# The first layer's attention segments in another order, with a refitted plan

## The chip, the cores and the metric

One core of one Trainium2 chip runs the whole kernel. The metric is device time in microseconds (us), the median of several runs.

## The reference

Four layers work on 2048 tokens of width 512 and add to x in turn: A, B, A, B, with the same weights both times. A is local attention (8 keys at distances 0, 2, ..., 14), B is full attention with 32 query heads that share one key head and one value head of width 16.

```python
x = A_x
x = x + _A_ref(_layernorm(x, axis=-1), A_wqkv, A_wo)
x = x + _B_ref(_layernorm(x, axis=-1), B_wq, B_wk, B_wv, B_wo)
x = x + _A_ref(_layernorm(x, axis=-1), A_wqkv, A_wo)
x = x + _B_ref(_layernorm(x, axis=-1), B_wq, B_wk, B_wv, B_wo)
...
scores = jnp.einsum("bhqd,bkd->bhqk", q, k) * (Dh ** -0.5)   # in _B_ref
p = _softmax(scores, axis=-1)
o = jnp.einsum("bhqk,bkd->bhqd", p, v)
```

## The kernel before, in words

The tokens are cut into four chunks of 512. "Layer" in the title means a pair A + B, numbered l = 0 and 1. For each chunk, `chunk` writes down the A part (layer norm, projections q, k, v, banded attention in "units", output projection) and then `b_in`, which makes B's keys (`kb`, into KAB) and queries (`qb`, into QT) of that chunk. These are operations with dependencies and estimated durations.

B's attention is a stream of tiles: one tile is 128 keys by 512 queries of one head group. A tile's scores are a matmul of 32 rows (line 1842). Its exponential is then taken by one of two engines: two tiles at a time on ACT (`exp`, line 1857, from a PSUM slot "st"), or one at a time on DVE (`copy`, line 1861, from a PSUM bank "dv", to a buffer t), from which POOL makes two shifted copies per tile (`do_pass`, line 1867). Then come matmuls with the values (line 1878), one for a tile that ACT took and three for a tile that DVE took. A tile may go either way, so ACT and DVE share the tile work.

The stream's order is written in `Net.order`. Each entry is (l, query chunk, key tiles), and it stands for eight segments, one for each pair (t, a) of head groups. When a query chunk meets its keys in several entries, the partial result of a segment is kept in X: the first part is copied out of PSUM (line 1897, DVE, or line 1895, ACT), every later part is added to X (line 1898, DVE alone). If another query chunk comes between, X goes to DRAM (line 1905) and comes back (line 1917). When a query chunk has met all keys, `rows` normalizes it, `out_rows` projects it, and its A part of the next layer is put into the plan.

A planner (`Sched.plan`) decides at build time in which order each engine issues all this. It takes for each engine the candidate with the smallest key: earliest start plus a bias. The biases (`PRM`, `Stream.BIAS`) are overridden from certain segments on by the table `PHASES`. `emit` writes the instructions in the planned order, and `chain` ties each to the one before on its engine. Some instructions are written without that tie: all but the last of the selects that build a band mask (`build_band_mask`, lines 1073 to 1079), and all but the last memset of `build_ones` (line 1094). Their place on POOL is decided when the program is built, around the tied ones.

DVE and POOL instructions that are marked with `port` are also tied to each other, across both engines, in the order of the plan: the later one waits for the earlier one by semaphore.

```python
if self.sched and self.sched.lock:
    order_after(self.tc, inst, self.tail.get("port" + {"dve": "pool", "pool": "dve"}[key]))
    self.tail["port" + key] = inst
```

Marked so are, in the start of the kernel: on DVE the layer norm's shift (line 1377), its normalization (line 1399) and the band mask of a unit (line 1585); on POOL the copies that spread A's values (line 1529).

Of the kernel before, what the change touches and what calls it, by code (L numbers as in the profile page):

```python
# [410 lines left out]
def outproj_tm(ctx, tc, o_tm, wo_sb, x_sb, ident, S, tag):  # L411
# [5 lines left out]
    for qt in range(NT):  # L417
# [27 lines left out]

PHASES = {
    0: ({
        "ex": -306.6, "add": 235.5, "vp": 291.7, "c3": -107.5, "dve": -147.3,
    }, {
        "dq": 159.2, "aq": -134.4,  # L450
    }),
    3: ({
        "age": 0.04278, "c2": -145.8,
    }, {
        "mmi": 48.87,
    }),
    6: ({
        "age": 0.05331,
    }, {
        "pv": 216.7, "mmpt": 17.28, "mmi": 4.008,  # L460
    }),
    9: ({
        "back": 1023,
    }, {
        "vec": 517, "mmi": -6.329, "aux": -147.2, "vec2": 217.1, "vech": 0.1986,
    }),
    12: ({}, {
        "few": 56.89, "slotv": 26.53,
    }),
    15: ({  # L470
        "age": 0.03159, "dve": -47.39,
    }, {
        "pv": 261.3, "copy": 144.9, "nt": -10.19, "mmpt": 38.35, "aux": -79.09, "exq": 23.25, "vecp": -40.88,
        "slotv": 38.3,
    }),
    18: ({
        "scale": 323.2,
    }, {}),
    21: ({}, {}),
    24: ({  # L480
        "recip": 623.4,
    }, {
        "batch": 20.29, "copy": -9.763,
    }),
    27: ({
        "scale": 268.7,
    }, {
        "npt": -0.5879, "ni": -9.215, "nt": 13.06, "mmq": 38.47,
    }),
    30: ({  # L490
        "age": 0.04279, "wpd": -0.07726, "mm_a": 405.5, "evacX": 93.91, "recip": 107.6, "c4": -43.8,
    }, {
        "pv": 222.9, "mmq": 11.47, "mmi": 42.58, "vec2": 155.6, "dq": -60.88,
    }),
    33: ({
        "age": 0.04061, "norm": 35.21, "aexp": -62.26, "ex": -204.6, "scale": -303.2, "dve": -86.78,
    }, {
        "vec": 419.9, "mmq": 7.941, "mmpt": 27.1, "mmi": 5.567, "aux": 49.57, "dq": 24.8,
    }),
    36: ({  # L500
        "age": 0.03932, "mm_a": 485, "norm": 69.12, "v0": 1080, "score": -231.1, "recip": 241.3, "scale": 350.2,
        "c5": 163.2,
    }, {
        "act": -182.5, "pv": 260.2, "npt": 3.996, "mmq": 38.14, "mmpt": -11.57, "mmi": 4.721, "vec2": 168.4,
        "vecp": -43.99, "slotv": 3.272,
    }),
    39: ({
        "age": 0.0403, "mask": -43.5, "c5": 75.84, "c6": 39.43,
    }, {
        "vec": 480.2, "batch": 23.44, "npt": 0.3429, "nt": -20.7, "mmq": 18.85, "mmpt": 25.18, "vec2": 184.8,  # L510
        "vecp": -74.21, "slotv": 31.5,
    }),
    42: ({
        "age": 0.04324, "mm_a": 502.6, "dmat": 736.3, "scale": 293.2, "c5": 79.56,
    }, {
        "vec": 466.2, "copy": 101.1, "ni": -11.61, "mmpt": 14.5,
    }),
    45: ({
        "age": 0.01627, "score": -187.1,
    }, {  # L520
        "pv": 267.3, "npt": 8.481, "nt": 11.16, "mmpt": 11.35, "mmi": 13.75, "aux": 15.46, "exq": -80.66,
    }),
    48: ({
        "mm_a": 410, "add": 91.46, "recip": 43.8, "c6": 51,
    }, {
        "pv": 276.6, "copy": 105.8, "npt": 2.948, "mmq": -2.49, "mmpt": 22.57, "mmi": 30.08, "vec2": 122.7,
        "dq": 38.09,
    }),
    51: ({
        "sc": 153.2,  # L530
    }, {
        "batch": 20.02, "ni": -21.41, "mmq": 8.641,
    }),
    54: ({}, {
        "aux": -58.57,
    }),
    57: ({
        "wd": 0.1189, "st": 130.9, "sc": 15.74,
    }, {
        "pv": 245.9, "batch": 19.21, "slotv": 20.79,  # L540
    }),
    60: ({
        "age": 0.041, "mm_a": 499.4, "act": 371.2, "dve": -34.12,
    }, {
        "vec": 446.8, "pv": 295.7, "pv_in": 180.4, "batch": 22.72, "npt": 30.29, "ni": -15.73, "nt": -40.24,
        "mmq": 6.584, "mmpt": 54.33, "mmi": 30.31, "exq": -41.21, "aq": -117.4, "vecp": -63.63,
    }),
    63: ({
        "act": -171.6,
    }, {  # L550
        "vec": 373.4,
    }),
    66: ({
        "recip": 149, "scale": 435,
    }, {}),
    69: ({
        "recip": 140.1,
    }, {
        "ni": -9.089, "nt": 22.53, "vecp": -73.11,
    }),  # L560
    72: ({
        "scale": 553.6,
    }, {
        "vec": 288.3, "pv": 129.3, "copy": 179.8, "vecp": 18.01,
    }),
    75: ({
        "mm_a": 483.7, "evacX": -26.18, "scale": 119.6,
    }, {
        "pv": 211.9, "npt": -16.9, "ni": -26.06,
    }),  # L570
    78: ({}, {}),
    81: ({
        "age": 0.04053, "mm_a": 487.1, "scale": 327.4,
    }, {
        "copy": 136.4, "ni": -11.35, "nt": -29.96, "mmpt": 87.33, "mmi": 4.607,
    }),
    84: ({}, {}),
    87: ({
        "mm_a": 54.57, "recip": 392.7,
    }, {  # L580
        "pv": 199.8, "vecp": -109.8,
# [12 lines left out]

# [532 lines left out]
class Net:  # L1127
# [1228 lines left out]
```

## Time and profile before

| what | us |
| --- | --- |
| median of 3 runs (lowest, highest) | 1377.09 (1376.57, 1378.69) |
| the profiled execution | 1378.62 |
| its span, first to last instruction | 1376.9 |
| busy: PE, ACT, DVE, POOL | 1340.7, 1318.4, 1292.0, 938.0 |

The profiled execution is 1.5 us over the median of the runs, and 1.7 us of it lie outside the span. Three engines are busy for 94% to 97% of the span. PE's share says less than it seems, since its matmuls overlap (up to four run side by side) and a busy PE may have room.

### The profile page before, as it was taken

Reading aid. Unit: us, or ns where it says so; the run is one execution under the profiler, and the core shown is the slowest. Engines: PE = TensorE matmul, PEld = TensorE weight load, DVE = VectorE, ACT = ScalarE, POOL = GpSimd, SP = SyncE. Lnnn points to the kernel's source line nnn. Section 1 sums busy time; section 2 is a strip of 40 time slices with the busy share of each in tenths; the row PEclk is TensorE's granted clock in tenths of the full one; section 3 lists DMA queues with packets and bytes.
Section 4 is the critical chain, followed back from the end, with each engine's and each line's share of the span. In section 5 each row is a group of like instructions: output and inputs, shape, how many; then the busy total and the mean of one; then the engine's idle time right before and its main releaser. Section 6 shows DMA issues by size and latency. Waiting matters only on the chain.

```text
span 1376.9 us, 48313 instructions
## 1 busy us (share of the span) xinstructions
PE 1340.7 (97%) x19729; PEld 455.5 (33%) x19729; DVE 1292.0 (94%) x2280; ACT 1318.4 (96%) x1593; POOL 938.0 (68%) x1225
## 2 busy tenths in 40 slices
PE   8999999999999999999999999999999999999996
PEld 5534343222224332433334333422222222222222
DVE  7988879999998899999999999899999999999996
ACT  7899989999999999999999999999999999999995
POOL 5137466788866657775668556677876778886884
PEclk9999999999999999999999999999999999999999
DMA  5012222011111110111101011121022200001000
GB/s 157 6 36 63 71 46 76 15 37 30 42 43 29 18 36 18 24 24 26 25 15 27 31 48 40 36 66 50 27 57 61 58 30 6 22 6 43 14 14 26
DMA packets 120014, 51.63 MB, mean 37 GB/s; under 512 B 98600, under 2 KB 104872, under 8 KB 119784
## 3 DMA queue, kind: packets, MB, share of 16 engines
q1 hardware_dynamic: 118920, 46.63, 13.7%
q8 instruction: 156, 2.56, 0.8%
q10 hardware_dynamic: 864, 1.84, 0.4%
q14 instruction: 74, 0.61, 0.1%
HBM read 22.90 MB, written 11.52 MB: 25 GB/s over the span
## 4 chain that ended last, share of the span: by engine, by line
PE 66%; ACT 17%; DVE 7%; POOL 5%; issue 4%; DMA 1%; SPq 0%; POOLq 0%; DVEq 0%; ACTq 0%
PE o L1878 28%; PE st L1842 22%; ACT pt L1857 14%; DVE t L1861 3%; PE y L1336 3%; PE qb L1336 2%; PE dv L1842 2%; ACT units L1857 2%; PE k L1336 2%; PE q L1336 2%; PE v L1677 2%; POOL i_pair L1867 1%; POOL i L1867 1%; POOL v L1693 1%; DMA region<-in_A_x_dram 1%
## 5 line engine op out<-in xcount | busy, mean ns | idle before, releaser
L1857 ACT ACTIVATE pt<-st 128x1024 bf16<-128x1024 f32 x1116 | 1076.6, 1125 | 19.4 <-PE dv L1842 11.0
L1861 DVE TENSOR_SCALAR t<-dv 128x512 int16<-128x512 f32 x1546 | 966.7, 681 | 29.4 <-PE dv L1842 24.3
L1867 POOL INT64_ADD i<-t x618 | 507.9, 829 | 250.9 <-DVE t L1861 80.3
L1867 POOL INT64_ADD i_pair<-t x414 | 340.5, 826 | 142.8 <-DVE t L1861 52.5
L1842 PE MATMUL st<-QT,KAB 32*128 32x512 bf16 x1300 | 252.5, 382 | 5.2 <-ACT pt L1857 2.4
L1842 PE MATMUL st<-QT,region 32*128 32x512 bf16 x1250 | 243.8, 381 | 5.6 <-ACT pt L1857 2.5
L1842 PE MATMUL dv<-QT,region 32*128 32x512 bf16 x798 | 244.2, 383 | 0.1
L1878 PE MATMUL o<-pt,VEa 128*32 128x512 bf16 x1138 | 235.9, 385 | 0.2 <-DVE t L1861 0.2
L1878 PE MATMUL o<-pt,region 128*32 128x512 bf16 x1094 | 235.2, 387 | 0.0
L1842 PE MATMUL dv<-QT,KAB 32*128 32x512 bf16 x748 | 232.3, 382 | 0.5 <-DVE t L1861 0.5
L1878 PE MATMUL o<-i,region 128*32 128x512 f16 x954 | 226.8, 386 | 0.3 <-POOL i L1867 0.3
L1878 PE MATMUL o<-t,region 128*32 128x512 f16 x798 | 207.0, 386 | 0.0
L1878 PE MATMUL o<-i,VEd 128*32 128x512 f16 x898 | 201.5, 384 | 0.1
L1878 PE MATMUL o<-t,VEd 128*32 128x512 f16 x748 | 196.1, 385 | 0.1
L1857 ACT ACTIVATE units<-st 128x1024 bf16<-128x1024 f32 x159 | 179.0, 1126 | 2.9 <-PE dv L1842 2.8
L1878 PE MATMUL o<-i_pair,region 128*32 128x512 f16 x642 | 170.2, 385 | 0.4 <-POOL i_pair L1867 0.4
L1842 PEld LDWEIGHTS <-region 32*128 32x128 bf16 x2048 | 81.0, 91 | 240.6 <-issue 236.6
L1842 PEld LDWEIGHTS <-KAB 32*128 32x128 bf16 x2048 | 78.0, 90 | 239.6 <-issue 233.2
L1878 PE MATMUL o<-i_pair,VEd 128*32 128x512 f16 x598 | 149.1, 384 | 0.1
L1878 PEld LDWEIGHTS <-region 128*32 128x32 f16 (+1 forms) x3644 | 71.0, 94 | 155.0 <-issue 150.8
L1878 PEld LDWEIGHTS <-VEd 128*32 128x32 f16 x2244 | 68.2, 94 | 81.6 <-issue 75.6
L1878 PEld LDWEIGHTS <-VEa 128*32 128x32 bf16 x1300 | 57.3, 94 | 60.8 <-issue 58.1
(193 smaller groups left out, 1268.7 us busy)
## 6 DMA issues: line engine op xcount, KB each, us to landing
xkd<-X SPq DMA_DIRECT2D x32, 256.0 KB
X<-xkd SPq DMA_DIRECT2D x32, 256.0 KB
lb<-rcd SPq DMA_DIRECT2D x31, 256.0 KB
X<-X SPq DMA_DIRECT2D x124, 32.0 KB
k<-oncA SPq DMA_DIRECT2D x96, 32.0 KB
w_sb<-in_A_wqkv_dram ACTq DMA_DIRECT2D x4, 384.0 KB
region<-in_A_x_dram SPq DMA_DIRECT2D x3, 512.0 KB
out_dram<-w_sb SPq DMA_DIRECT2D x3, 512.0 KB
```

The costliest lines, as they stand in the source:

```text
L1336: self.chain("pe", self.nc.tensor.matmul(st["ps"][g:g + 32], lhsT=lhsT[:, g:g + 32], rhs=rhs, start=first and n == 0, stop=last and n == l ...
L1677: self.chain("pe", nc.tensor.matmul(ps[0][32 * h:32 * h + 32, b], lhsT=B.xnT.t[:, kt, at:at + 32], rhs=wv[:, kt, h, :, :], start=(kt == 0) ...
L1693: self.chain("pool", nc.gpsimd.tensor_copy(out=vv[rows, 4 * n:4 * n + 4, :, 16 * h:16 * h + 16].rearrange("p b g d -> p (b g) d"), in_=st. ...
L1842: self.chain("pe", self.nc.tensor.matmul(out, lhsT=self.KAB[l][32 * g:32 * g + 32, a, kt * 128:(kt + 1) * 128], rhs=self.QT[32 * g:32 * g ...
L1857: self.chain("act", self.nc.scalar.activation(out=self.pt[pt][:, 0:n, :], in_=self.st.pop(key)[:, 0:n, :], func=AF.Exp, scale=E_SCALE))
L1861: self.chain("dve", self.nc.vector.tensor_scalar(out=self.t[buf][:, r, :].bitcast(I16), in0=self.dv[bank][:], scalar1=-U_BIAS, scalar2=U_B ...
L1867: self.chain("pool", self.nc.gpsimd.int64_add(words(self.i[out]), words(self.t[buf]), J_OFF[j] * 0x0001000100010001))
L1878: self.chain("pe", self.nc.tensor.matmul(self.o[bank][32 * g:32 * g + 32, :], lhsT=lhsT, rhs=rhs, start=first, stop=last, tile_position=(0 ...
```

## The change

The order of segments of the first layer's first two query chunks is another one. Before: chunk 0 on keys 0, chunk 1 on keys 0 and 1, chunk 0 on keys 1 to 3, chunk 1 on keys 2 and 3. After: chunk 0 on keys 0, chunk 0 on keys 1, chunk 1 on keys 0 to 2, chunk 0 on keys 2 and 3, chunk 1 on keys 3. There is one entry more, so eight segments more, and the segment numbers behind it move up by eight. The table PHASES has other numbers throughout, those in force from the first instruction on among them. The new table is 29 lines longer, so line n of the kernel before that stands behind it is line n + 29 after.

```diff
 PHASES = {
     0: ({
-        "ex": -306.6, "add": 235.5, "vp": 291.7, "c3": -107.5, "dve": -147.3,
+        "norm": 328.5, "vcopy": 15.72, "ln": -57.44, "ex": -364.2, "on": 22.28, "c1": -185.7, "c3": -110.5,
+        "vfirst": -1066, "dve": -150.6,
     }, {
...
     def order(self):
         k = lambda a, b: range(4 * a, 4 * b)
-        return [(0, 0, k(0, 1)), (0, 1, k(0, 2)), (0, 0, k(1, 4)), (0, 1, k(2, 4)),
+        return [(0, 0, k(0, 1)), (0, 0, k(1, 2)), (0, 1, k(0, 3)), (0, 0, k(2, 4)), (0, 1, k(3, 4)),
                 (0, 2, k(0, 4)), (0, 3, k(0, 4)),
                 (1, 0, k(0, 2)), (1, 1, k(0, 3)), (1, 0, k(2, 4)), (1, 1, k(3, 4)), (1, 2, k(0, 4)), (1, 3, k(0, 4))]
```

**First place: POOL in the start, where A's values of chunk 0 are spread.** Line 1529 (1558 after) copies the values, two instructions for each of four blocks. `bandones` is the pattern for the narrow band mask (line 1073: its memset, 1077 and 1079: its selects), `ones` a constant. Before:

```order
L1529 COPY v<-oncA 64x32x16 x2
L1094 MEMSET ones_114 32x16 x3
L1529 COPY v<-oncA 64x32x16 x4
L1073 MEMSET bandones 128x40
L1529 COPY v<-oncA 64x32x16 x2
L1077 AFFINE_SELECT bandones<-bandones 32x8
L1077 AFFINE_SELECT bandones<-bandones 32x32
```

After:

```order
L1558 COPY v<-oncA 64x32x16 x2
L1123 MEMSET ones_114 32x16 x3
L1102 MEMSET bandones 128x40
L1106 AFFINE_SELECT bandones<-bandones 32x8
L1106 AFFINE_SELECT bandones<-bandones 32x32
...
L1108 AFFINE_SELECT bandones<-bandones 32x8
L1558 COPY v<-oncA 64x32x16 x6
L1567 COPY ks<-k 128x512
```

The memset and 15 selects stood behind all eight copies (the memset behind six), and stand now between the second copy and the third.

**Second place: DVE at the same time.** Line 1311 (1340) casts values, 1084 (1113) makes the wide band mask's bits, 1377 (1406) is the layer norm's shift for chunk 1, 1399 (1428) normalizes rows of chunk 1 (to a borrowed buffer `pt`), 1313 (1342) scales keys, 1416 (1445) copies transposed rows, 1585 (1614) masks the first unit. The brackets name the semaphores that an instruction waits for. Before:

```order
L1311 CAST oncA<-v 128x512 [waits PE_49] x3
L1084 TENSOR_SCALAR bandmask_102<-bandones 128x72 [waits Pool_49]
L1377 SCALAR_TENSOR_TENSOR sm_201<-sm_201 128x2 [waits DVE_49,Activation_49,Pool_49]
L1311 CAST q_183<-q 128x512 [waits PE_49]
L1313 TENSOR_SCALAR k<-k,kmask 128x8x64 [waits PE_49]
L1416 COPY QT<-pT 128x4x128 [waits PE_49] x2
L1585 TENSOR_TENSOR units<-units,bandmask_102 128x576 [waits DVE_49,Activation_49,Pool_49]
```

After:

```order
L1340 CAST oncA<-v 128x512 [waits PE_49]
L1113 TENSOR_SCALAR bandmask_102<-bandones 128x72 [waits Pool_49]
L1406 SCALAR_TENSOR_TENSOR sm_201<-sm_201 128x2 [waits DVE_49,Activation_49,Pool_49]
L1428 TENSOR_SCALAR pt_157<-region,sm_201 128x512 [waits DVE_49]
L1428 TENSOR_SCALAR pt_157<-region,sm_201 128x512 [waits Pool_49]
L1340 CAST q_183<-q 128x512 [waits PE_49]
L1342 TENSOR_SCALAR k<-k,kmask 128x8x64 [waits PE_49]
L1445 COPY QT<-pT 128x4x128 [waits PE_49] x2
L1614 TENSOR_TENSOR units<-units,bandmask_102 128x576 [waits DVE_49,Activation_49,Pool_49]
```

Two casts went to ACT, and two normalizations came from ACT. By the counts that the semaphores are waited for, the shift waited for the sixth copy on POOL and waits now for the second; the second normalization is new here and waits for the fourth copy; the unit's mask waits for the eighth copy in both; the third copy waits for the first normalization, the fifth for the second.

**Third place: ACT while the A part of chunk 3 projects q and k** (line 1308, 1337 after: casts of the projections; line 1857, 1886 after: exponentials). Before:

```order
L1857 ACTIVATE pt_155<-st 128x1024
L1308 CAST oncA<-k 128x2x256
L1857 ACTIVATE pt_154<-st 128x1024
L1308 CAST oncA<-k 128x2x256
L1308 CAST q_184<-q 128x512
L1308 CAST oncA<-k 128x2x256
L1308 CAST q_185<-q 128x512
L1308 CAST oncA<-k 128x2x256
L1857 ACTIVATE pt_157<-st 128x1024
```

After:

```order
L1337 CAST oncA<-k 128x2x256
L1886 ACTIVATE pt_155<-st 128x1024
L1886 ACTIVATE pt_154<-st 128x1024
L1337 CAST q_184<-q 128x512
L1886 ACTIVATE pt_157<-st 128x1024
L1886 ACTIVATE pt_158<-st 128x1024
L1337 CAST q_185<-q 128x512
L1337 CAST oncA<-k 128x2x256
L1886 ACTIVATE pt_156<-st 128x1024
```

Of the eight projections, the last six stood on PE in one piece without a score between them (five of their casts follow each other on ACT); now the last three do, and exponentials stand between the others.

## Rows read from the trace of the kernel before

**Rows 1.** The page: its span, and busy time of each engine with its share.

```profile
span 1376.9 us, 48313 instructions
PE 1340.7 (97%) x19729; PEld 455.5 (33%) x19729; DVE 1292.0 (94%) x2280; ACT 1318.4 (96%) x1593; POOL 938.0 (68%) x1225
```

**Rows 2.** Stretches: length, busy us of PE, PEld, DVE, ACT, POOL, clock, DMA.

```profile
123.00:230.50 107.50, 104.96 (x2092) 41.77 (x2080) 90.09 (x165) 102.04 (x138) 64.05 (x91) 1.00 0.24 58
411.50:750.00 338.50, 334.63 (x5512) 118.21 (x5504) 320.73 (x559) 329.76 (x394) 229.86 (x296) 1.00 0.12 24
750.00:967.00 217.00, 213.22 (x3399) 73.39 (x3396) 202.78 (x355) 210.46 (x257) 146.28 (x188) 1.00 0.17 45
280.00:320.00 40.00, 39.19 (x418) 10.74 (x414) 39.99 (x68) 40.00 (x45) 32.79 (x41) 1.00 0.13 38
```

**Rows 3.** The chain that ended last, 13 to 40 us: start, us, what.

```profile
17.81 0.62 POOL v L1529
...
18.65 0.81 ACT pt L1396
...
21.98 0.88 PE k L1336 x16
...
25.38 0.68 DVE units L1585
```

**Rows 4.** Timeline of POOL in the start: start, us, line, operation, tiles, [idle before].

```profile
14.02 1.27 POOL L1529 COPY v<-oncA 64x512 bf16<-64x512 bf16 x2 [6.36 <-DVE sm L1377]
15.35 0.46 POOL L1094 MEMSET ones<- 32x16 bf16 x3
15.85 2.57 POOL L1529 COPY v<-oncA 64x512 bf16<-64x512 bf16 x4
...
20.02 1.84 POOL L1077 TENSOR_SCALAR_AFFINE_SELECT bandones<-bandones 32x8 bf16<-32x8 bf16 x7
...
22.44 1.29 POOL L1079 TENSOR_SCALAR_AFFINE_SELECT bandones<-bandones 32x32 bf16<-32x32 bf16 x6
```

**Rows 5.** Timeline of DVE in the start.

```profile
13.79 1.88 DVE L1311 CAST oncA<-v 128x512 bf16<-128x512 f32 x3
15.58 0.17 DVE L1084 TENSOR_SCALAR bandmask<-bandones 128x72 int16<-128x72 bf16 x1
18.45 0.16 DVE L1377 SCALAR_TENSOR_TENSOR sm<-sm 128x2 f32<-128x2 f32 x1 [2.69 <-POOL v L1529]
18.53 0.69 DVE L1311 CAST q<-q 128x512 bf16<-128x512 f32 x1
19.13 0.74 DVE L1313 TENSOR_SCALAR k<-k,kmask 128x512 bf16<-128x512 f32 x1
...
20.60 0.79 DVE L1585 TENSOR_TENSOR units<-units,bandmask 128x576 int32<-128x576 int32 x1
21.32 0.44 DVE L1399 TENSOR_SCALAR pt<-region,sm 128x512 bf16<-128x512 bf16 x1
```

**Rows 6.** Timeline of PE in the start.

```profile
21.54 0.31 PE L1594 MATMUL oa<-units,v 128*32 128x72 bf16 x16
...
21.80 1.05 PE L1336 MATMUL k<-xnT,w_sb 128*32 128x512 bf16 x16
```

**Rows 7.** Timeline around chunk 3's projections: PE's weight loads, and DVE.

```profile
173.70 4.87 PEld L1336 LDWEIGHTS <-w_sb 128*32 128x32 bf16 x96 [0.23 <-issue]
...
179.42 1.89 DVE L1861 TENSOR_SCALAR t<-dv 128x512 int16<-128x512 f32 x3 [3.92 <-PE dv L1842]
```

**Rows 8.** Timeline around three projections in one piece (chunk 2): ACT and DVE.

```profile
97.07 0.59 ACT L1308 CAST oncA<-k 128x512 bf16<-128x512 f32 x1 [0.95 <-PE k L1336]
...
98.74 0.69 DVE L1311 CAST oncA<-k 128x512 bf16<-128x512 f32 x1 [1.74 <-PE k L1336]
```

**Rows 9.** Groups of instructions by line: the additions to X.

```profile
L1898 DVE TENSOR_TENSOR X<-X,o 128x512 f32<-128x512 f32 x32 | 21.7, 678 | 0.0
```

**Rows 10.** Two stretches near the end, columns as in group 2.

```profile
1256.00:1258.00 2.00, 1.19 (x10) 0.47 (x8) 2.00 (x3) 2.00 (x3) 0.64 (x1) 1.00 0.04 12
1258.00:1260.00 2.00, 2.00 (x22) 0.46 (x22) 1.60 (x4) 1.81 (x3) 0.00 (x0) 0.65 0.00 0
```

More of the change, by code (lines that the diff above doesn't have):

```diff
@@ L476 @@
     18: ({
-        "scale": 323.2,
-    }, {}),
-    21: ({}, {}),
+        "mask": 63.94, "ex": -87.79, "vp": 114.7, "dve": -49.74,
+    }, {
+        "pv_in": 163.8, "batch": 12.75, "few": 14.25, "ni": 0.5239, "mmi": 30.09, "vec2": 24.51, "dq": -77.6,
+        "vecp": -77.63, "acth": 0.1808,
+    }),
+    21: ({
+        "age": 0.007666, "wd": 0.04937, "mm_a": 491.6, "c3": -378.6, "dve": 290.4,
+    }, {
+        "pv": 226, "pv_in": 213, "batch": 14.25, "npt": -1.638, "ni": -24.63, "nt": 11.69, "mmq": -2.301,
+        "mmpt": 29.33, "mmi": 25.71,
+    }),
     24: ({
-        "recip": 623.4,
+        "recip": 0.3494,
     }, {
-        "batch": 20.29, "copy": -9.763,
+        "ni": -65.91,
     }),
@@ L486 @@
         "scale": 268.7,
+    }, {}),
+    30: ({
+        "age": 0.08271, "recip": 107.6, "scale": 190.9,
     }, {
-        "npt": -0.5879, "ni": -9.215, "nt": 13.06, "mmq": 38.47,
+        "vec": 555.7, "pv": 263.4, "batch": 22.05, "copy": 51.08,
     }),
[L490 to L498, printed above, removed]
+    33: ({}, {
+        "copy": 175.8, "npt": 38.04, "ni": -88.23,
@@ L499 @@
     }),
     36: ({
-        "age": 0.03932, "mm_a": 485, "norm": 69.12, "v0": 1080, "score": -231.1, "recip": 241.3, "scale": 350.2,
-        "c5": 163.2,
-    }, {
-        "act": -182.5, "pv": 260.2, "npt": 3.996, "mmq": 38.14, "mmpt": -11.57, "mmi": 4.721, "vec2": 168.4,
-        "vecp": -43.99, "slotv": 3.272,
+        "age": 0.03496,
+    }, {
+        "act": -153.5, "vec": 502.9, "copy": 196.9,
     }),
     39: ({
-        "age": 0.0403, "mask": -43.5, "c5": 75.84, "c6": 39.43,
+        "age": 0.04164, "wd": 0.071, "mm_a": 383.1, "v0": 1157, "score": 100.9, "recip": 140.8,
@@ L515 @@
     }, {
-        "vec": 466.2, "copy": 101.1, "ni": -11.61, "mmpt": 14.5,
+        "act": -154.5, "pv": 194.4, "batch": 16.41, "mmpt": 183.2,
     }),
[L518 to L521, printed above, removed]
+    45: ({}, {
+        "copy": -30.15,
     }),
     48: ({
-        "mm_a": 410, "add": 91.46, "recip": 43.8, "c6": 51,
+        "age": 0.03117, "wpd": -0.1019, "mm_a": 267.2, "v0": 993.6, "mask": 29.63, "p0": -93.83, "ln": -286.6,
@@ L525 @@
     }, {
-        "pv": 276.6, "copy": 105.8, "npt": 2.948, "mmq": -2.49, "mmpt": 22.57, "mmi": 30.08, "vec2": 122.7,
-        "dq": 38.09,
+        "vec": 430, "pv_in": 254.5, "batch": 15.54, "copy": 151.9, "ni": -30.95, "mmq": 33.36, "mmpt": -32.32,
+        "mmi": 21.86, "vec2": 176.5, "vecp": -64.44, "slotv": 29.37,
     }),
     51: ({
-        "sc": 153.2,
+        "sc": 153.2, "mask": -20.51,
     }, {
-        "batch": 20.02, "ni": -21.41, "mmq": 8.641,
+        "pv_in": 154.3, "batch": 20.24, "ni": -21.41, "mmq": 8.641,
@@ L547 @@
     }),
     63: ({
-        "act": -171.6,
+        "wpd": -0.02581, "p0": -79.14, "act": -164.5,
     }, {
-        "vec": 373.4,
+        "vec": 360.6, "pv_in": 193.3, "batch": 20.59, "npt": -4.892, "mmq": -0.5585, "vec2": 177.6,
+        "vecp": -42.62, "slotv": 14.42, "vech": -0.1368,
     }),
     66: ({
-        "recip": 149, "scale": 435,
-    }, {}),
+        "age": 0.03238, "mm_a": 329.7, "norm": 484.3, "score": -296.6, "on": 45.58, "c7": 27.87,
+    }, {
+        "act": -96.52, "vec": 439.5, "copy": 76.88, "npt": -16.81, "ni": 2.671, "nt": -11.06, "mmq": 5.539,
+        "mmi": 22.99, "vec2": 132, "vecp": -49.22, "slotv": 7.495,
+    }),
@@ L587 @@
     }),
     93: ({
+        "recip": 381, "scale": 449.5,
+    }, {
+        "vec": 498.8, "ni": -30.23, "nt": -8.103,
+    }),
+    96: ({
+        "age": 0.03791, "mm_a": 459.1, "recip": 71.68,
+    }, {
+        "vec": 530.1, "pv": 321, "batch": 21.84, "copy": -136.1, "mmq": 16.3, "mmi": 151, "vec2": 98.72,
+    }),
+    99: ({
+        "age": 0.02015, "mm_a": 116.6, "mm_b": -1116, "recip": 343.7, "scale": 53.21,
+    }, {
+        "vec": 358.7, "batch": 19.29, "few": 40.14, "mmq": 33.28, "mmpt": 53.79, "mmi": 151, "slotv": -21.82,
+    }),
```

88 lines of the change are left out of this document (49 added, 39 removed).

## The prediction

> **What bounds the kernel now.** I read the busy times of the page first: PE, ACT and DVE are all over 93% [rows 1], so no single engine is the answer, and the next view has to be one by stretches. In a stretch of pure attention (280 to 320 us) ACT is busy 40.00 of 40 us and DVE 39.99 [rows 2]. There the two engines that take the tiles are the bound, together: an exponential on ACT costs 40.00 / 45 = 0.89 us, an instruction on DVE 39.99 / 68 = 0.59 us, and PE, with its overlapping matmuls, keeps up. Work added to either engine there lengthens the run by about half of itself, because the planner can move tiles to the other.
>
> In the stretches that hold the A parts it is different. From 123 to 230.5 us, where chunks 2 and 3 of the first layer are made, DVE is idle for 107.5 - 90.1 = 17.4 us and ACT for 5.5; from 411.5 to 750 us for 17.8 and 8.7, and from 750 to 967 us for 14.2 and 6.5 [rows 2]. Part of that idle time has a plain cause: when PE does several projections in one piece, no scores come out, and both engines run dry. Six projections in one piece (96 weight loads, 4.87 us) left DVE waiting 3.92 us for its next scores [rows 7]; three in one piece cost DVE 1.74 and ACT 0.95 us in their longest waits [rows 8].
>
> The start is bound by neither. The chain of work that ended last runs there through one engine after the other: POOL's copies of the values, a normalization on ACT, a projection on PE, a unit's mask on DVE [rows 3]. Whatever is late here makes everything behind it late.
>
> **The start: a wait on POOL, +3.6 us.** In the kernel before, POOL copies the values of two blocks at 14.02 and 15.85 and following, and DVE's shift waits for it 2.69 us, until 18.45 [rows 4, 5]. After the change, the memset and the 15 selects for the narrow mask, which nothing needs for a long time, stand on POOL between the second copy and the third, and DVE's second normalization waits for the fourth copy. I follow both engines with the durations of before.
>
> POOL: the first two copies end at 14.02 + 1.27 = 15.29, the small memsets at 15.81 [rows 4]. DVE's one remaining cast takes a third of 1.88 us from 13.79 on, so the mask bits are made by about 14.6, and the memset that waits for them is not held up [rows 5]. From about 15.85 come the memset and the selects. The selects took 22.44 + 1.29 - 20.02 = 3.71 us before [rows 4]; the memset, which stands between rows, took 0.1 to 0.2 us. So they end at about 19.8. Copies three and four take 1.27 us as the first two did, to 21.1.
>
> DVE: its shift now needs the first two copies only and runs at 15.4, the first normalization ends before 15.9 at 0.44 us [rows 5]. The second waits until 21.1 and ends at 21.55. POOL's last four copies wait for it, and take 2.57 us [rows 4], to 24.2. The cast of q, which started at 18.53 before, starts at 21.55; the scaling of k and two copies follow, and the unit's mask, at 20.60 before [rows 5], waits for POOL's eighth copy, until 24.2. That is 3.6 us late.
>
> What is late next: the multiplication with the values on PE, which waited for this mask until 21.54, and behind it in PE's order the projection of k at 21.80 [rows 6], which is on the chain at 21.98 [rows 3]. DVE has statistics, aggregates and the next scaling behind the mask, and was itself on the chain at 25.38 [rows 3]. So PE, DVE and ACT all move by 3.6 us at a point where the run is one chain; the selects' own 3.71 us on POOL cover nothing later. I carry the full 3.6 on to the end: instructions keep a fixed order, so a later start of the stream moves all of it. The bounds are 0, if slack that I don't see takes it up, and 3.6 + 2.6 (the rival on the clock, below). The gain at this place, that the shift no longer waits 2.69 us, is in the sum already.
>
> **The eight segments more, +2.4 us.** Each new part of a segment is added to X on DVE; the 32 additions of before took 0.68 us each with their overlap [rows 9], and I price them as any DVE instruction at 0.59. Counted in the two orders over the whole program, DVE gets 8 additions, 4 tile copies, one copy of X and one normalization more, and 7 casts less: (8 + 4 + 1 - 7) x 0.59 + 0.44 = +4.0 us [rows 2, 5]. ACT gets 2 exponentials and one normalization (0.81 us [rows 3]) less, and 6 net casts and copies more at up to 0.59 us [rows 8]: -1.8 - 0.8 + 3.5 = +0.9 us. Shared by two saturated engines this is 4.9 / 2 = +2.4 us. Bounds: 0 if it all fills idle time, +4.0 if DVE alone ends last. PE's 8 matmuls more are 0.04% of its 19729 instructions [rows 1]; partial results go to DRAM and back as often as before, in transfers that no row of the chain waits for.
>
> **Chunk 3's A part is spread, -1.3 us; later stretches, +0.9 us.** Before, chunk 0 needs the third key chunk 16 tiles after it meets the second, so chunk 3 has to be finished by the 420th tile or so; its last query projection stands at tile 434 in PE's order. After, those keys are first needed at tile 656, and that projection stands at tile 531. The piece of six projections is gone. It cost DVE 3.92 us in one wait [rows 7], and about 2 more on both engines around it by the same view, so 6 / 2 = 3.0. In its place stands a piece of three, which by the waits in [rows 8], with the smaller ones beside them, costs (1.74 + 1.75) / 2 = 1.7. Together -1.3. Key chunk 2 is needed earlier, at tile 288 and not 400, but its last projection stands at tile 256, some 32 tiles ahead, so I see no wait there. In the later A parts the refitted plan has one piece of three projections where there was none; its 1.7 us stand against slightly fewer changes between score and value matmuls on PE (2574 instead of 2609), so I take half, +0.9. The bounds for all idle time together are wide: -11.4, if the whole idle time of 123 to 230.5 us went (17.4 + 5.5, halved), and about +3.
>
> **Sum.** 3.6 + 2.4 - 1.3 + 0.9 = +5.6 us on the span of 1376.9, so 1382.5 us. The profiled execution lasted 1378.62, the runs 1377.09 in the median; I carry the difference over to the median: **1382.7 us**.
>
> **Rivals.** *PE's clock falls in the new gap.* Before, PE has work at 21.54 and 21.80 [rows 6]; after, it has almost none between its projection of q and about 25.1, when the mask comes. Near the end of the trace PE was busy 1.19 of 2.00 us at a granted clock of 1.00, and in the next two microseconds it was granted 0.65, so part of them at 1.2 GHz [rows 10]. If that follows here, the three projections behind the gap (0.88 us each [rows 3]) take twice as long: +2.6, 1385.3 us. Against it: one place is little evidence, and what stood ahead of it there was not a gap alone. The Trainium skill, "TensorE: Matmul & The Clock Gate", section "Why this matters for your kernels", asks to avoid idle gaps between bursts of matmuls, because the clock then drops to half; by that rule this rival would be the forecast, and the trace agrees with it in the one place of group 10. Chance 0.18.
>
> *The start hides the wait.* Chunk 1's work, which DVE does in between, could be what was ahead of need, and the lateness be lost in waits that I read as fixed. For it: DVE waited there before, too. Against it: PE and DVE are both on the chain within 5 us of the mask. Then only 2.0 remain: 1379.1 us. Chance 0.22.
>
> *The spread pays more than it costs.* If the projections of chunk 3 no longer starve the two engines at all between 123 and 230.5 us, the gain is 11.4 and not 1.3, and the sum with the start and the additions is 3.6 + 2.4 - 11.4 = -5.4: 1371.7 us. It decides from 6.0 us on, over half of that idle time. Against it: every A part has such idle time, also where its projections are spread (14.2 and 6.5 us for 750 to 967 us [rows 2]). Chance 0.10.
>
> **Numbers.** The forecast has 0.50, its own range is 1380 to 1385. The range for 8 in 10 goes from 1376 to 1386.5: it takes in the hidden start and the slower clock, and leaves out most of the last rival. A measurement of this kernel can tell about 0.2%, 2.8 us, from no change. Faster by more than that is the last rival, nearly alone: 0.10. Within it lie most of the hidden start and the low end of the forecast: 0.23. Slower: 0.67.
>
> **What would show it.** In the profile after, DVE should wait for POOL's copies in the start some 5 us, from about 15.9 to 21.1, and PE's first value matmul stand at about 25.1 instead of 21.54. The first scores of the stream should be 3 to 4 us later than before. DVE's busy time should be about 4 us more and ACT's about 1. The idle time of DVE around chunk 3's projections should show no wait over 2 us. If the first scores come as early as before, the start is wrong; if they come late and the end does not, idle time later took it up; a granted clock under 1.00 before 30 us is the rival on the clock.

## The result, and the profile after

The changed kernel takes 1385.07 us in the median of 4 runs (1384.5 to 1386.21), the kernel before 1377.89 in 4: a ratio of 1.0055, 95% interval 1.0043 to 1.0067. It is slower by 7.2 us. The forecast was 1382.7, 5.6 over the median shown. The result lies in the range for 8 in 10 (1376 to 1386.5), just above the forecast's own range (1380 to 1385), and within 0.3 us of what the rival on the clock named (1385.3). The profiled execution lasted 1384.97 us.

The first lines of the page answer to [rows 1]. DVE has 2.6 us more work and ACT 0.9, so most of the 5.7 us that the span grew is waiting.

```profile
span 1382.6 us, 48310 instructions
PE 1343.4 (97%) x19737; PEld 458.1 (33%) x19737; DVE 1294.6 (94%) x2287; ACT 1319.3 (95%) x1596; POOL 937.7 (68%) x1227
```

To find where, I cut both spans at the same points of the work: the last tile of the first entry, the last tile of the first two query chunks in the first layer, the last tile of the second layer's entry on chunk 1 and key chunks 0 to 2, the last tile of all. Columns as in [rows 2]; after, then before:

```profile
0.00:126.00 126.00, 115.84 (x2592) 58.85 (x2594) 101.21 (x231) 104.66 (x181) 49.32 (x103) 0.97 0.20 53
126.00:414.50 288.50, 284.06 (x4037) 91.97 (x4032) 272.32 (x476) 281.92 (x336) 201.55 (x261) 1.00 0.20 49
414.50:974.50 560.00, 549.74 (x8896) 193.04 (x8896) 524.06 (x919) 538.53 (x650) 378.33 (x487) 1.00 0.14 32
974.50:1367.00 392.50, 386.75 (x4194) 111.24 (x4192) 388.63 (x646) 390.77 (x426) 306.73 (x377) 1.00 0.11 31
1367.00:1382.60 15.60, 7.06 (x42) 3.04 (x37) 8.38 (x19) 3.40 (x8) 1.76 (x2) 0.83 0.12 38
```

```profile
0.00:122.00 122.00, 113.91 (x2592) 57.21 (x2594) 104.06 (x234) 103.02 (x179) 49.52 (x103) 1.00 0.25 67
122.00:411.50 289.50, 284.52 (x4072) 93.89 (x4060) 269.54 (x472) 283.44 (x339) 201.88 (x260) 1.00 0.18 45
411.50:967.00 555.50, 547.85 (x8905) 191.61 (x8897) 523.50 (x914) 540.22 (x650) 376.14 (x484) 1.00 0.14 32
967.00:1359.00 392.00, 387.00 (x4154) 109.74 (x4155) 386.51 (x648) 388.26 (x423) 308.44 (x378) 1.00 0.11 30
1359.00:1376.90 17.90, 7.42 (x44) 3.09 (x36) 8.36 (x17) 3.44 (x8) 2.00 (x3) 0.84 0.10 34
```

Length less busy time is idle time. Taken as the mean of ACT and DVE, as the prediction did, the five stretches and the work add up to the 5.7 us:

| part | idle before, ACT / DVE | idle after | mean difference |
| --- | --- | --- | --- |
| start, first entry | 19.0 / 17.9 | 21.3 / 24.8 | +4.6 |
| rest of the first two query chunks, first layer | 6.1 / 20.0 | 6.6 / 16.2 | -1.6 |
| up to the last tile on second-layer keys 0 to 2 | 15.3 / 32.0 | 21.5 / 35.9 | +5.1 |
| pure attention behind it | 3.7 / 5.5 | 1.7 / 3.9 | -1.8 |
| behind the last tile | 14.5 / 9.5 | 12.2 / 7.2 | -2.3 |
| work of ACT and DVE (+0.9 / +2.6) | | | +1.8 |

**The start.** POOL, answering to [rows 4]: the selects stand ahead of the third copy, which starts at 19.32.

```profile
13.85 1.27 POOL L1558 COPY v<-oncA 64x512 bf16<-64x512 bf16 x2 [6.20 <-DVE sm L1406]
...
17.97 1.29 POOL L1108 TENSOR_SCALAR_AFFINE_SELECT bandones<-bandones 32x32 bf16<-32x32 bf16 x6
19.32 1.28 POOL L1558 COPY v<-oncA 64x512 bf16<-64x512 bf16 x2
21.18 2.59 POOL L1558 COPY v<-oncA 64x512 bf16<-64x512 bf16 x4 [0.58 <-DVE pt L1428]
```

DVE, answering to [rows 5]: the second normalization waits 4.99 us for those copies, and the unit's mask moves from 20.60 to 23.80.

```profile
20.63 0.41 DVE L1428 TENSOR_SCALAR pt<-region,sm 128x512 bf16<-128x512 bf16 x1 [4.99 <-POOL v L1558]
...
23.80 0.76 DVE L1614 TENSOR_TENSOR units<-units,bandmask 128x576 int32<-128x576 int32 x1 [0.84 <-POOL v L1558]
...
29.87 0.75 DVE L1342 TENSOR_SCALAR k<-k,kmask 128x512 bf16<-128x512 f32 x1 [2.32 <-PE k L1365]
```

PE, answering to [rows 6], and its clock in stretches of 2 us. The value matmuls come at 24.71 instead of 21.54, and the three projections behind them follow each other in 1.66 to 1.70 us, not in 0.87: the granted clock is 0.50. It falls between 21 and 23 us (0.79 in that stretch), behind PE's wait of 1.95 us that ended at 21.10, and the second wait, of 1.16 us, already lies in the half clock. DVE's next scaling of k, at 24.63 before, comes at 29.87, 5.2 us late.

```profile
21.10 0.40 PE L1439 MATMUL pT<-ident,pt 128*128 128x128 bf16 x4 [1.95 <-DVE pt L1428]
...
24.71 0.42 PE L1623 MATMUL oa<-units,v 128*32 128x72 bf16 x16 [1.16 <-DVE units L1614]
25.18 1.90 PE L1365 MATMUL k<-xnT,w_sb 128*32 128x512 bf16 x16
26.84 1.95 PE L1365 MATMUL q<-xnT,w_sb 128*32 128x512 bf16 x16
28.54 1.27 PE L1365 MATMUL k<-xnT,w_sb 128*32 128x512 bf16 x16
```

```profile
21.00:23.00 2.00, 1.70 (x20) 0.70 (x20) 1.96 (x5) 0.66 (x1) 1.72 (x3) 0.79 1.03 330
23.00:25.00 2.00, 0.84 (x40) 0.60 (x40) 1.20 (x3) 1.68 (x4) 0.72 (x2) 0.50 0.35 124
27.00:29.00 2.00, 2.00 (x27) 0.78 (x22) 0.54 (x5) 0.86 (x2) 0.00 (x0) 0.50 0.01 4
29.00:31.00 2.00, 1.74 (x40) 0.88 (x32) 1.13 (x2) 2.00 (x5) 0.00 (x0) 1.00 0.00 0
```

**The second layer's A parts.** In the third stretch of the table the loss is concentrated in two places. Compared at the same count of tiles that have their exponential, the mean idle time of ACT and DVE grew by 4.0 us from the 2048th tile to the 2200th, and by 2.7 us from the 2350th to the 2500th (862 to 922 us, 855 to 913 before); in the rest of the stretch it shrank by 1.7. The first of the two places, after and before:

```profile
748.20:811.60 63.40, 60.98 (x1357) 25.55 (x1354) 54.57 (x99) 59.31 (x82) 39.52 (x54) 1.00 0.16 36
```

```profile
750.80:807.00 56.20, 54.67 (x894) 19.61 (x881) 52.65 (x101) 54.90 (x73) 32.99 (x45) 1.00 0.16 41
```

The changed kernel has a whole chunk's projections in it. From 750 to 780 us its DVE is busy 22.5 of 30 us and ACT 26.8:

```profile
750.00:760.00 10.00, 10.00 (x147) 3.56 (x147) 7.13 (x12) 9.14 (x12) 3.16 (x4) 1.00 0.08 17
760.00:770.00 10.00, 9.89 (x231) 4.11 (x233) 9.13 (x15) 9.83 (x12) 8.07 (x11) 1.00 0.32 58
770.00:780.00 10.00, 8.01 (x313) 4.91 (x313) 6.21 (x11) 7.83 (x14) 5.89 (x10) 1.00 0.09 29
```

PE and DVE there: three projections with no scores between, for which DVE waits 2.61 us, then value projections of many small matmuls, for which it waits 2.36 us, and waits of PE itself marked "issue".

```profile
756.91 1.04 PE L1365 MATMUL k<-xnT,w_sb 128*32 128x512 bf16 x16
757.77 1.04 PE L1365 MATMUL q<-xnT,w_sb 128*32 128x512 bf16 x16
758.64 1.04 PE L1365 MATMUL k<-xnT,w_sb 128*32 128x512 bf16 x16
...
771.13 0.95 PE L1706 MATMUL v<-w_sb,xnT 128*32 128x128 bf16 x53 [0.42 <-issue]
```

```profile
760.13 1.50 DVE L1890 TENSOR_SCALAR t<-dv 128x512 int16<-128x512 f32 x2 [2.61 <-PE dv L1871]
...
772.13 0.69 DVE L1340 CAST xn<-v 128x512 bf16<-128x512 f32 x1 [2.36 <-PE v L1706]
```

### The profile page after: what moved, and what is told of

It reads as the page before. It is cut to its first block, busy times and chain, and to the rows that moved or that the text cites. A ratio compares the mean times of both kernels' runs of the same rounds, so it can differ in the third digit from the quotient of the medians.

```text
span 1382.6 us, 48310 instructions
## 1 busy us (share of the span) xinstructions
PE 1343.4 (97%) x19737; PEld 458.1 (33%) x19737; DVE 1294.6 (94%) x2287; ACT 1319.3 (95%) x1596; POOL 937.7 (68%) x1227
## 4 chain that ended last, share of the span: by engine, by line
PE 70%; ACT 20%; issue 4%; DVE 3%; POOL 3%; DMA 0%; POOLq 0%; SPq 0%; ACTq 0%; DVEq 0%
PE o L1907 29%; PE st L1871 23%; ACT pt L1886 15%; PE y L1365 4%; ACT units L1886 3%; PE qb L1365 2%; PE dv L1871 2%; PE q L1365 2%; PE k L1365 2%; PE v L1706 2%; DVE t L1890 1%; POOL i L1896 1%; POOL i_pair L1896 1%; PE kb L1365 1%; PE oa L1786 1%
## 5 line engine op out<-in xcount | busy, mean ns | idle before, releaser
L1907 PE MATMUL o<-pt,region 128*32 128x512 bf16 x1098 | 238.5, 385 | 0.4 <-DVE t L1890 0.4
L1871 PE MATMUL dv<-QT,KAB 32*128 32x512 bf16 x758 | 235.4, 382 | 0.2 <-DVE t L1890 0.2
L1907 PE MATMUL o<-i,region 128*32 128x512 f16 x950 | 219.6, 385 | 0.1
L1907 PE MATMUL o<-i,VEd 128*32 128x512 f16 x913 | 206.6, 385 | 0.1
L1907 PE MATMUL o<-t,VEd 128*32 128x512 f16 x758 | 202.9, 385 | 0.0
L1907 PE MATMUL o<-i_pair,region 128*32 128x512 f16 x634 | 165.0, 385 | 1.7 <-POOL i_pair L1896 1.7
```

The source lines that it names most:

```text
L1871: self.chain("pe", self.nc.tensor.matmul(out, lhsT=self.KAB[l][32 * g:32 * g + 32, a, kt * 128:(kt + 1) * 128], rhs=self.QT[32 * g:32 * g ...
L1907: self.chain("pe", self.nc.tensor.matmul(self.o[bank][32 * g:32 * g + 32, :], lhsT=lhsT, rhs=rhs, start=first, stop=last, tile_position=(0 ...
```

## The experiments

Twelve kernels ran in three series, each beside runs of the kernel before on its own chip. Medians of before differ between chips (1377.85, 1375.71, 1377.49 us), so each run is told as its difference to those. Where two runs' intervals overlap, their difference is not clear of noise.

| run | median us | to before | ratio, 95% interval |
| --- | --- | --- | --- |
| after_selects_late | 1384.17 | +6.3 | 1.0045 (1.0033, 1.0057) |
| after_filled_gaps | 1389.17 | +11.3 | 1.0082 (1.0068, 1.0096) |
| before_selects_early | 1381.92 | +4.1 | 1.0027 (1.0017, 1.0037) |
| after_old_start_weights | 1383.54 | +5.7 | 1.0038 (1.0024, 1.0052) |
| before_longer_warmup | 1375.51 | -0.2 | 1.0002 (0.9993, 1.0011) |
| after_longer_warmup | 1385.51 | +9.8 | 1.0067 (1.0054, 1.0081) |
| after_late_selects_longer_warmup | 1384.92 | +9.2 | 1.0068 (1.0054, 1.0082) |
| before_eight_more_segments | 1436.25 | +60.5 | 1.0445 (1.0429, 1.0461) |
| after_selects_in_gap | 1389.11 | +11.6 | 1.0083 (1.0065, 1.0102) |
| before_new_start | 1381.69 | +4.2 | 1.0027 (1.0015, 1.0039) |
| after_half_projections | 1374.50 | -3.0 | 0.9974 (0.9963, 0.9986) |
| before_half_projections | 1368.12 | -9.4 | 0.9934 (0.9915, 0.9953) |

Kernels whose DVE and ACT orders are the same can be laid over each other instruction by instruction. The difference of the start times ("lead") then shows where time is won and lost, much finer than a median does.

### The start alone

**Selects late in the new order.** Each of the selects is chained on POOL, so that they run where the plan has them:

```diff
-wide = self.op("pool", 2500.0, lambda op: self.chain("pool", w.select(32)), [self.bits], after=32000.0, prio=LATER)
+wide = self.op("pool", 2500.0, lambda op: w.select(32, lambda i: self.chain("pool", i)), [self.bits], after=32000.0, prio=LATER)
```

> The changed kernel, with the memset and the 16 selects of the narrow mask tied to their planned place on POOL, behind all the copies of the values; PE, ACT, DVE and SP keep their order word for word. Theory (the start carries most of the loss): DVE's second normalization of chunk 1 runs at about 17 us instead of 20.63, the first unit's mask at about 20.3 instead of 23.80, PE has no gap of more than 1 us and a granted clock of 1.00 through the start, and the run ends 5 us earlier than the changed kernel, at 1380 (ratio to before 1.001 to 1.003). Rival (the start's delay is taken up by later slack, and the eight segments and the refitted plan make the loss): the start is as early, and the run still takes 1384 to 1386.

It won 0.9 us on the change, not clear of noise and far from 5, so the theory failed as stated. Its trace had a fault of its own: the granted clock was 0.60 from 11 to 13 us and 0.54 from 13 to 15, behind a wait of 2.58 us at PE's first transpositions (1.99 in the changed kernel, at 1.00). Counted from the first projection of q, the mask came after 22.04 - 16.89 = 5.2 us and not after 23.80 - 14.93 = 8.9. The second series therefore kept PE busy up to there:

```diff
-        for _ in range(17):
+        for _ in range(24):
             self.idle_matmul(warm, (128, 128), 512, True)
```

> The kernel before, with 24 idle matmuls on PE ahead of the program's first transpositions instead of 17, and no other change on PE, ACT, DVE and SP. In the first series the profiles showed the granted clock at 0.5 for 3.41 us from about 11 us on, behind a wait of 2.3 to 2.6 us at the first transpositions; in the profile of the kernel before that wait was 1.42 and the clock stayed at 1.00. Theory (this fall is an accident that hits some runs of every kernel and costs about 1.5 us): the wait is under 1 us, the clock 1.00 at 11 us, the median 0 to 1.5 us below before, 1376.3 to 1377.8, with less scatter. Rival (it costs nothing): the same as before. This run is the base for the other three of its series.

> The changed kernel, with the same 24 idle matmuls. Theory: no fall at 11 us, the fall at 22 us stays, since it comes from the wait on POOL; 1384 to 1385. It is the base for the run with the selects late.

> The changed kernel, with the selects behind the copies and the 24 idle matmuls. Theory (the start costs 3.5 us by the wait and 1.5 by the clock, and the first series hid it behind the fall at 11 us): 3.5 to 5 us below the changed kernel with the longer warm-up, 1379.5 to 1381. Rival (the start costs about 1 us, as the first series had it): 0.5 to 1.5 us below, 1383 to 1384, and the loss of 6 us that remains lies in the order, the segments and the later plan.

The clock stayed at 1.00 at 11 us in all of them, and the longer warm-up is worth nothing in the median (-0.2). With the selects late the lead over the changed kernel with the same warm-up was 4.78 us at 30 us, but only 1.80 at 60 and 0.62 at the end. Its trace shows what took most of it back: the selects now stand between POOL's later copies, a mask on DVE waits for those, and PE's clock falls behind that wait (0.56 from 41 to 43 us).

```profile
40.38 0.76 DVE L1614 TENSOR_TENSOR units<-units,bandmask 128x576 int32<-128x576 int32 x1 [2.11 <-POOL KAB L1558]
```

**Selects in POOL's idle time.** The third attempt put them behind the eighth copy, in the third series:

```diff
+                self.spreads += 1
+                if self.spreads == 4:
+                    self.masks = self.w.steps(32)
+                    for _ in range(16):
+                        self.chain("pool", next(self.masks))
```

> The changed kernel with the longer warm-up, and the memset and 15 selects directly behind the eighth copy of the values, where POOL has nothing to do from 23 to 31 us; PE, ACT, DVE and SP keep their order. The earlier run put them between POOL's later copies for chunk 1, and in its trace a lead of 4.8 us at 30 us had shrunk to 1.8 at 60 us, because a mask on DVE then waited 2.11 us for those copies at about 43 us. Theory (the start's delay is carried to the end, the earlier place only moved it): the lead over the changed kernel with the longer warm-up is 4.5 to 5 us at 30, at 60 and at 700 us, and the run ends at 1380 to 1381.5. Rival (later slack takes up what the start loses): a lead of 5 us at 30 us again shrinks, and the run ends at 1384 to 1385.

> The kernel before with the longer warm-up, with the change's weights for the first segment alone, and the selects directly behind the eighth copy. Old order, old weights from segment 3 on. Theory (the refitted start is not worse than the old one, only the selects in it are): the first unit's value matmuls come 0.5 to 1 us earlier after the first projection than before, and the run takes 0 to 1 us less than before. Rival (the refitted start is itself the loss): 3 us or more above before.

The second takes the change's weights for the first segment, and the same place for the selects:

```diff
 PHASES = {
-    0: ({"ex": -306.6, "add": 235.5, "vp": 291.7, "c3": -107.5, "dve": -147.3}, {"dq": 159.2, "aq": -134.4}),
+    0: ({"norm": 328.5, "vcopy": 15.72, "ln": -57.44, ...}, {"dq": 156.1}),
```

Neither tested what it was made for: chained inside an operation that is tied to DVE, the selects became what the unit's mask waits for.

```profile
23.67 0.76 DVE L1621 TENSOR_TENSOR units<-units,bandmask 128x576 int32<-128x576 int32 x1 [3.80 <-POOL bandones L1109]
```

So the mask was as late as in the changed kernel (at 23.99 in the run in the old order, 20.60 before), and PE's clock fell again (1.66 us from one projection to the next). That makes of the second one a test of the other direction: in the old order, a mask that is 3.4 us late costs 4.2 us at the end. The run with the selects early says the same.

```diff
             def spread(op, k2=k2, stage=stage):
+                if B is self.sets[0] and c == 0 and self.spreads == 1:
+                    self.masks = self.w.steps(32)
+                    for _ in range(16):
+                        self.chain("pool", next(self.masks))
+                self.spreads += 1
```

> The kernel before, with the memset and 15 of the 16 selects moved ahead of the third copy of the values on POOL, where the changed kernel has them; PE, ACT, DVE and SP keep their order word for word. Theory: DVE's shift that ran at 18.45 us now waits until about 21, the first unit's mask moves from 20.60 to 23 or later, PE gets a gap and its clock may fall; the run ends 3 to 5 us later, at 1381 to 1383. Rival (later slack takes it up): 1378, as before.

The narrow pattern is written here before the wide mask is read from it, so this kernel's wide masks, and its outputs, are others. The unit's mask came 24.44 - 16.36 = 8.1 us after the first projection of q, and not 20.60 - 14.75 = 5.9, so 2.2 us late; the projections behind it were at half clock, two of them 0.8 us longer each; and the run ended 4.1 us later. In the old order the start's delay is carried on whole: laid over the kernel before, this run is 6.6 us late at 30 us (3.8 of them at 18 us already, behind a fall of its clock at 11 us) and 6.9 at 1000 us, and the run with the new start's weights 4.8 and 5.0. Behind 1000 us both win 2.2 us back, 1.3 to 1.4 of it where the trace of before has a fall of the clock [rows 10] and theirs have none.

```profile
22.29 0.16 DVE L1379 SCALAR_TENSOR_TENSOR sm<-sm 128x2 f32<-128x2 f32 x1 [2.50 <-POOL v L1536]
...
25.85 1.88 PE L1338 MATMUL k<-xnT,w_sb 128*32 128x512 bf16 x16
27.51 1.92 PE L1338 MATMUL q<-xnT,w_sb 128*32 128x512 bf16 x16
```

**The old start in the new order.** One entry of the table of weights:

```diff
 PHASES = {
-    0: ({"norm": 328.5, "vcopy": 15.72, "ln": -57.44, ...}, {"dq": 156.1}),
+    0: ({"ex": -306.6, "add": 235.5, "vp": 291.7, "c3": -107.5, "dve": -147.3}, {"dq": 159.2, "aq": -134.4}),
```

> The changed kernel, with the first three segments planned by the weights of the kernel before (the entry for segment 0 alone) and all later weights those of the change; the selects then fall behind the copies by themselves. New order and eight segments more are kept. Theory: the start is that of before (mask at 20.6 us, clock 1.00), and 5 us are won against the changed kernel: 1380. Rival (order and segments make the loss): 1384 to 1386. Well under 1379 would mean that the new order itself costs nothing or gains.

It won 1.5 us, not 5, and this is not clear of noise. Its start is as good as before's, though its own clock had fallen at 11 us: value matmuls 6.1 us after the first projection (22.38 - 16.32; 6.8 before). Laid over the changed kernel by its exponentials it leads by 4.1 us at 68 us and by 4.1 still at 189, by 3.1 from 270 on, by 2.8 at 757, by 0.1 at 799 and by 1.4 at the end. So in the new order, too, nothing in the stream takes the start's delay up. The lead was lost in two short places, and at both PE ran at half clock in this trace. In the second PE had also waited 3.0 us on "issue" (0.64, 0.80 and 1.56, told in the last section), all of it before the clock fell:

```profile
229.30:232.70 3.40, 3.40 (x84) 1.63 (x85) 2.66 (x5) 3.01 (x6) 0.83 (x1) 0.50 0.02 5
778.90:782.30 3.40, 3.40 (x63) 1.04 (x56) 1.90 (x4) 3.07 (x5) 2.81 (x5) 0.50 0.06 11
```

**The clock alone.** Idle matmuls fill the two gaps of PE in the changed kernel's start; the waits on POOL stay.

```diff
+                    if c == 1 and i == 1:
+                        self.fill(op, 9)
                     pT = self.psum(op, [128, 4, 128], BF16, "pT")
...
+            if (c, t, kd) == (0, 0, 0):
+                self.fill(op, 5)
             o = state["o"] = self.bank[op.buf].tile([128, 2, 256], F32, name="oa", tag="bk")
```

> The changed kernel, with nine idle matmuls of 512 columns on PE ahead of chunk 1's second transposition and five ahead of the first unit's value matmuls, which fill the two gaps of 1.95 and 1.16 us; the waits on POOL stay. Theory (gap first, then half a clock, both paid): the granted clock stays 1.00, the value matmuls still start at about 24.7 us, the projections behind them follow each other in 0.87 us and not in 1.66, so that the third ends 1.6 to 2.0 us earlier; the run ends about 1.7 us earlier, at 1383.4. Rival (DVE and ACT are so late that PE's half clock costs nothing): 1385. If the clock falls all the same, the idle matmuls are not what it asks for.

At the place itself it did what was expected: the clock stayed at 1.00, and the three projections took 2.8 us (26.36 to 29.14) instead of 4.6 (25.18 to 29.81), so the clock's price is 1.8 us. The run as a whole was 4 us slower. By the lead, it lost 0.7 us around 233 us, 1.0 between 600 and 640, 3.6 from 721 to 781 and 1.3 around 885; at 783 PE waited 2.21 us for nothing that the profile shows, and the clock fell behind it. The wait ends at a packet of PE's instructions (last section). Fourteen more instructions near the start move the points at which packets end; whether that is why these places are worse is open.

```profile
782.82 0.41 PE L1772 MATMUL st<-q,k 64*128 64x40 bf16 x14 [2.21 <-issue]
```

```profile
782.80:786.20 3.40, 3.38 (x39) 1.11 (x38) 1.36 (x3) 2.02 (x3) 1.33 (x2) 0.50 0.03 7
```

### Eight more segments

```diff
-        return [(0, 0, k(0, 1)), (0, 1, k(0, 2)), (0, 0, k(1, 4)), (0, 1, k(2, 4)),
+        return [(0, 0, k(0, 1)), (0, 1, k(0, 2)), (0, 0, k(1, 2)), (0, 0, k(2, 4)), (0, 1, k(2, 4)),
```

> The kernel before with the 24 idle matmuls and its third entry cut in two: the first query chunk on key chunk 1, then on 2 and 3, in the old order, so eight more segments, closes and additions to X, with the weights of the later segments moved up by eight. Forecast's step (eight segments cost 2.4 us): 2.4 above before with the longer warm-up, bounds 0 and 4. Rival (the segments are the whole of what the start does not explain): 5 to 6 above.

The end says nothing about segments: behind 415 us the planner, whose weights were fitted to other segments and only moved up by eight, makes a plan with long waits. Up to there it can be read. The entries ahead of the cut end at the same time as in the kernel before with the longer warm-up (230.3 and 230.2 us), and the last of the three key chunks at 340.3 instead of 337.0:

```profile
230.30:340.30 110.00, 108.94 (x1164) 31.93 (x1163) 107.37 (x180) 108.79 (x120) 81.52 (x101) 1.00 0.15 34
```

```profile
230.20:337.00 106.80, 105.09 (x1173) 30.55 (x1172) 105.14 (x177) 106.38 (x118) 84.90 (x105) 1.00 0.14 37
```

Eight more segments cost 3.2 us: 2.2 on DVE and 2.4 on ACT as work, and 0.8 to 1.0 more waiting on each. It is one execution of each kernel.

### The second layer's projections

Both kernels with half of the contraction left out in the second layer's projections:

```diff
         def run(some, first, last):
+            some = some[:1] if thin else some
...
-                        for kt in range(4):
+                        for kt in (0, 3) if thin else range(4):
```

> The changed kernel with the longer warm-up, leaving out half of the contraction (two of four blocks) in the second layer's projections of q, k and v, so that its outputs are not the reference's: 768 of PE's matmuls, some 22 us of its time by the durations of this case (0.054 us for a projection's matmul, 0.016 for a value's), and nothing on another engine. Theory (in the changed kernel a second-layer chunk's projections stand so close together, from about 752 to 780 us, that PE cannot feed ACT and DVE, which lose some 5 us more there than before): 5 to 8 us less than the changed kernel. Rival (those waits come from the fixed order or from POOL, not from PE's work): 0 to 3 less.

> The kernel before with the longer warm-up and the same half of the second layer's projections left out (its outputs are not the reference's either). Theory (its projections are spread better, so PE's work is mostly hidden): 1 to 3 us less than before, so 3 to 5 less gained than in the changed kernel. Rival: the same gain in both.

The changed kernel gained 9.8 + 3.0 = 12.8 us and the kernel before 9.4 - 0.2 = 9.2; by the spans 1383.6 - 1372.2 = 11.4 and 1374.5 - 1366.3 = 8.2. Both gained more than expected, so PE's work in the A parts is far from hidden in either kernel, but the changed one gained 3.2 to 3.6 us more, as the theory had it. The intervals of the medians leave that difference open; the lead shows where it lies. Against the same kernel with the longer warm-up, 5.3 us of the changed kernel's gain fall between 721 and 781 us (3.8 against the changed kernel itself), and no wait on "issue" is left there; the kernel before gains 0.2 us there, and at most 3.1 in any 60 us (804 to 863). The third stretch of the table without that work, after and before: ACT's idle time is now 13.5 and 9.7 us, DVE's 28.6 and 27.9, and the mean difference 2.2 instead of 5.1. So leaving it out takes away 2.9 us of the 5.1 (5.3 of 7.6, at the same counts of tiles, against the two profiles with the longer warm-up), and 2.2 stay unexplained. The edit also leaves out 768 weight loads, so it does not tell PE's busy time from the number of its instructions.

```profile
414.50:964.50 550.00, 535.37 (x8131) 180.69 (x8130) 521.39 (x920) 536.54 (x651) 378.75 (x487) 1.00 0.15 33
```

```profile
411.50:959.00 547.50, 534.01 (x8145) 180.38 (x8141) 519.59 (x915) 537.82 (x651) 376.44 (x485) 1.00 0.15 33
```

## Why the prediction was right, and where it was not

**The start (+3.6 forecast).** The steps came as described: DVE waits from 15.6 to 20.63, the mask is 3.2 us late, the value matmuls 3.2. The rival on the clock (+2.6, chance 0.18) was no rival but came on top: PE's gap was followed by half a clock, worth 1.8 us at that place, and the start's idle time rose by 4.6. The stream's first exponential starts at 68.28 us and not at 63.32, so 5.0 us late, where 3 to 4 had been named. The Trainium skill, "TensorE: Matmul & The Clock Gate", section "Why this matters for your kernels", warns of idle gaps between bursts of matmuls, behind which the clock drops to half. The trace agrees that such a fall comes behind a gap (0.50 behind the one of 1.95 us), but this gap is shorter than those that the page warns of. That the delay is carried on is shown in the old order (+4.1 and +4.2 at the end); in the new order it is shown up to 757 us, and taking the delay away brought only 0.9 to 1.5 us in the medians, and by the lead the runs without it lost time later: around 230 us, and where the second layer's A parts stand.

**Eight segments (+2.4).** Under-sized: 3.2 measured, within the bounds. The work in it, 2.3 us as the mean of the two engines, is what the term named; the 0.9 us of waiting was not in it. In the whole kernel ACT's work came as counted (+0.9), and DVE's to +2.6, not +4.0.

**The spread of chunk 3 (-1.3).** -1.6 by the idle time of its stretch, in which some waiting for the new segments also falls. DVE's waits around chunk 3's projections are under 1.4 us, as forecast (3.92 before).

**Later stretches (+0.9).** This step failed. The working looked for pieces of three or more projections without scores and found one. The idle time of the stretch with the second layer's A parts rose by 5.1 us, and the half projections show that PE's work there, as busy time or as number of instructions, is the cause of 2.9 of them, or of more: not the one piece alone, but a whole chunk's projections and values, packed into some 30 us. The other 2.2 stay open.

**What the sum left out.** The pure attention behind 967 us waits 1.8 us less (before had a fall of the clock there [rows 10]; after has none, and three kernels in the old order without it gain 1.3 to 1.4 us on before at that place), and the end behind the last tile is 2.3 us shorter. These 4.1 us happen to cancel the 4.2 that the later stretches were short of, so the sum of 5.6 for a growth of 5.7 is better than its terms: that is luck. The median grew by more than the profiled executions did, 7.2 us against 6.4, and that it came out where the clock's rival had it is luck as well, since that rival has the forecast's other terms.

Still open: what the start costs at the end in the new order. No run has the selects wholly out of the way; the nearest, with the old start's weights, won 1.5 us in the median and led by 4.1 in the trace up to 189 us. Nor did any run that does the whole work beat the kernel before: the longer warm-up, the only such edit of it that cost nothing, gave nothing.

## What to carry to other kernels

An instruction that only its last sibling is tied to can be moved by the build into a gap that is none: look for such loose instructions on an engine that others wait for, and when tying them, look at what the tie itself makes wait. Price a moved stage by how dense its work stands beside the stream, over tens of microseconds, and not by its longest piece. And lay traces of kernels with the same order over each other, since a median hides that one place wins 4 us and two others lose them. Where many small matmuls stand close, count PE's instructions as well as its time.

## What was not expected of the hardware

PE waits at times for nothing that the profile shows ("issue"), and above all where small matmuls stand close. From 770 to 780 us it had 313 matmuls and as many weight loads in 10 us, against 147 from 750 to 760. Such waits of over 0.35 us between 765 and 785 us: 0.42 and 0.49 in the changed kernel; 0.78, 0.53 and 2.14 with the longer warm-up; 0.64, 0.80 and 1.56 with the old start's weights; one to three, of 0.70 to 2.21, in the four others in the new order that do the whole work; none with half the projections, none there in the kernel before.

The traces' records of DMA packets tell what PE waits for. Two pages, of the changed kernel and of the one with half the projections (packets, MB, share):

```profile
q8 instruction: 156, 2.56, 0.8%
```

```profile
q8 instruction: 150, 2.46, 0.8%
```

Leaving out 768 matmuls and as many weight loads takes 6 packets off this queue, so it brings PE's instructions, and a packet holds 1536 / 6 = 256 of them. All 86 waits of PE on "issue" of over 0.35 us between 12 and 1360 us, in all fourteen kernels, end 1.19 to 1.61 us after one of these packets has landed. In the changed kernel packets land at 769.90, 773.54 and 777.74 us, and PE goes on at 771.13, 774.88 and 779.09, at instructions that are 256 apart (the third wait, of 1.04 us, the profile puts down to ACT). So PE waits there for its next instructions. In the third stretch of the table such waits of over 0.35 us are 1.2 us before and 3.5 after.

The changed kernel and the one with the longer warm-up have the same instructions there, so what such a place costs differs from execution to execution, and the clock fell behind it in four of the seven profiles in the new order that have the whole work.

The granted clock fell behind waits of PE at other places too, in some of the profiles and not in others that have the same instructions there (at about 11, 230, 780, 880 and 1257 us). A fall cost 1.8 us among projections in the start, which is the chain, and 0.7 to 0.9 us at 230 us.

The end behind DVE's last instruction took 8.0 us in the kernel before (1368.9 to 1376.9) and 5.5 in the changed one (1377.1 to 1382.6). It took 7.6 to 8.1 us in the five kernels with the old segments, 5.5 to 5.7 in the eight in the new order, and 5.9 in the old order with eight segments more. No work of the kernel stands in it, so 2.3 to 2.5 us of any comparison of the first two come from there. In the traces' packet records, the five with the long end have 87 packets on the second queue that carries instructions (queue 14), all others 86, and the last of the 87 starts within 0.2 us of the end; that this packet makes the difference was not tried.
